# Batch 0 of a fused attention and FFN kernel in another order: x in halves, w_out's quarters right behind w_in's, batch 1 turned in blocks

## The chip, the core and the metric

The kernel runs on one core of a Trainium2 chip. The metric is the device time of one execution in microseconds, the median of the runs; lower is better. A core has five engines with a queue each: TensorE (PE, matrix products, into the PSUM memory of eight banks), VectorE (DVE), ScalarE (ACT), GpSimd (POOL) and SyncE (SP, which issues most of the DMAs here). Each works through its own list in order and waits on semaphores for the others.

## What is computed

```python
# x (8, 8, 512, 64), state (8, 8, 32, 64): batch, head, tokens, width
scores = scale * x @ state^T ; a = softmax(scores)        # rows over 32 states
xread  = a @ state                                        # (8, 8, 512, 64)
scores2 = scale * state @ x^T ; a2 = softmax(scores2)     # rows over 512 tokens
sread  = a2 @ x                                           # (8, 8, 32, 64)
h = concat(xread, sread) as (8 * 544, 512)                # heads side by side
out = elu(h @ w_in) @ w_out        # w_in 512 x 2048, w_out 2048 x 512, float32
```

Each of the 8 batches has 512 token rows and 32 state rows of the FFN's input. All data are float32. In the kernel the raw 64-bit words of the weights are rebuilt into float32 by a few bit operations on ACT and DVE before use.

## The kernel before, in words

**Reassociation.** `a @ state @ w_in` is computed as `a @ (state @ w_in)`: `make_m` (M) makes the small matrix m for a chunk of 512 columns, in two groups `g` of heads, and `ffn1` (F) multiplies it with aT, the turned softmax. So the first FFN product of one of the 16 column blocks `fo` is two matmuls (k = 0, 1) of 128x512, and the second one (`ffn2_row`, O) in batch 0 is four, accumulated over all `fo` in banks 0 to 3. ELU lies between: two ACT steps (`exp_part`, R) and one DVE step (`max_part`, E).

**Batch 0** is written out by hand in `first_batch` as a plan, a string of steps; every engine keeps the order of the plan. The steps that the text names: `x:b.i` turns half i of x of batch b on PE into PSUM (`turn_x`), `xc` copies it out, `sc` makes the scores (`scores`); `mx`, `tr`, `ae`, `tm`, `ps`, `te`, `su`, `pm`, `tt`, `sd` are the two softmaxes, of which `ps` and `pm` are on POOL, `ae` and `te` on ACT, the others on DVE; `tt` makes aT. `sT` and `sTc` turn the other softmax on PE and copy it to aT_s, `sr` is the product a2 @ x (`state_read`), `src` its copy. `w:k.1` and `w:k.2` convert weight tile k, first on ACT, then on DVE. `Z:n` are n products of the identity that nobody reads. `kU` and `kUc` turn and copy the states of the other batches. There are 32 weight tiles of 0.5 MB; `fetch` issues their loads on SP, 7 ahead, and after them x of batch 1 and four DMAs of 1 MB that write the finished w_in to memory (`w_in_mem`), from where later batches read back the part of w_in that is overwritten. Before, the tiles come in the order w_in chunk 0, w_in chunk 1, w_out 0 to 3, w_in chunk 2, and so on. At the end of the plan, batch 1 gets its scores and softmax in the same way as batch 0.

**Batches 1 to 7** run through `batch(b)`: 16 times F and ELU, with make_m for chunks 2 and 3 at `fo` = 5, and then a Strassen scheme (`Strassen`, `Second`) for the second product, whose sums of operands are made on DVE (`whole.sums()`: one written over g_all, then s). Between the Strassen products the hooks run the attention of the next batch: scores (s1), then `move_state`, which turns blocks of 32x32 on DVE into a_blocks and moves them with sixteen DMAs to aT_s, and six products later `state_read`. In these batches x comes in a second form too: `load_blocks` loads 32x32 blocks with sixteen DMAs, and `turn_blocks` turns them on DVE into xT_b. `weight_sum` and `Second.weights` make sums of weights in batch 1; two of the tables lie over the space of w_in's chunks 2 and 3, once these are used and written out.

**Order.** A recording layer, `InOrder`, marks each instruction as kept in program order while its engine's `on` is set; otherwise a scheduler may move it. ACT and POOL are kept for batch 0, SP and PE all the way, DVE (`vector`) up to a line `vector.on = False` in `batch`. x lies in one buffer (`xpool`), so x of a batch can be loaded only after state_read of the one before. Blocks of x, xT of batch 0 and the output tiles share two buffers (`opool`); weight tiles, aT_s, a_blocks, xT_b and the sums share eleven (`work`).

Of the kernel before, what the change touches and what calls it, by code (L numbers as in the profile page):

```python
# [25 lines left out]
def kernel(  # L26
# [103 lines left out]

    x_t, st, m_t = {}, {}, {}

    def load_x(b, engines):
        x_t[b] = xpool.tile([P, R, DM], FP32, name="x_sb")
        x_v = x[b].rearrange("h (p r) d -> p r h d", r=R)
        for r in range(R):
            engines[r % len(engines)].dma_start(
                out=x_t[b][:, r].rearrange("p (h d) -> p h d", d=D), in_=x_v[:, r]
            )

    def load_blocks(b):

# [16 lines left out]
    def turn_blocks(b, m):  # L159

        i, j = divmod(m, 2)
        if j == 0:
            st[b, "xT", i] = work.tile([P, 2, R * P], FP32, tag="w", name="xT_b")
        st[b, m] = st[b, "xT", i][:, j]
        vector.transpose(st[b, m], st[b, "blocks", i][:, j])
# [18 lines left out]
        return raw  # L184

    def turn_states(raw, b0, b1):
        ps = st["k_ps"] = pair(6)[:, :, : (b1 - b0) * 64].rearrange("p t (b q) -> p t b q", q=64)
        for b in range(b1 - b0):
            transpose(ps[:, :, b], raw[:, b].rearrange("p c d -> p (c d)"))

# [14 lines left out]
    def high_words(raw):  # L205
        return raw.bitcast(U32).rearrange("p n (j w) -> p n j w", w=2)[:, :, :, 1]

    def convert_1(dst, raw):

        lo, hi = low_words(raw), high_words(raw)

        scalar.activation(
            out=lo.bitcast(FP32), in_=lo, func=AF.Copy, scale=2.0**-29, bias=2.0**23
        )
        scalar.activation(out=lo, in_=lo.bitcast(FP32), func=AF.Copy, bias=-(2.0**23))


        scalar.activation(out=dst, in_=hi.bitcast(FP32), func=AF.Abs)  # L220

    def convert_2(dst, raw):
        lo, hi = low_words(raw), high_words(raw)
        vector.tensor_scalar(
            out=dst, in0=dst, scalar1=as_float(896 << 20),
            scalar2=as_float((1151 << 20) - 1), op0=ALU.max, op1=ALU.min,
        )

        bits = dst.bitcast(U32)
        vector.tensor_scalar(  # L230
            out=bits, in0=bits, scalar1=3, scalar2=0x3FFFFFF8,
            op0=ALU.logical_shift_left, op1=ALU.bitwise_and,
        )
        vector.scalar_tensor_tensor(
            out=bits, in0=hi, scalar=0xC0000000, in1=bits,
            op0=ALU.bitwise_and, op1=ALU.bitwise_or,
        )
        vector.tensor_tensor(out=bits, in0=bits, in1=lo, op=ALU.add)
# [18 lines left out]
                transpose(ps[:, :, j, r], x_t[b][:, r, m * P : (m + 1) * P])  # L257
        st[b, "xT", i] = ps

    def copy_x(b, i):  # L260
        xT = opool.tile([P, 2, R * P], FP32, tag="o", name="xT")
        for j in range(2):
            st[b, 2 * i + j] = xT[:, j]
            scalar.copy(
                out=xT[:, j].rearrange("p (r t q) -> p t r q", t=2, q=64),
                in_=st[b, "xT", i][:, :, j],
            )

    def by_state(b, rhs, first=6):

# [147 lines left out]
    def make_m(b, c, h=None, first=6):  # L418

        c_in = c if b < 2 else c % 2  # L420
        halves = slice(2 * c_in, 2 * c_in + 2) if h is None else slice(2 * c_in + h, 2 * c_in + h + 1)
        assert h is None or b == 0
        st[b, "m", c] = by_state(b, [w_in[:, halves, m] for m in range(NP)], first)

    def copy_m(b, c, g, copy):
        if g == 0:
            m_t[b, c] = mpool.tile([P, G, 512], FP32, name="m_sb")
        copy(out=m_t[b, c][:, g], in_=st[b, "m", c][:, g])

    def copy_half(b, c, h):  # L430
        if h == 0:
            m_t[b, c] = mpool.tile([P, G, 512], FP32, name="m_sb")
        scalar.copy(
            out=m_t[b, c][:, :, h * 256 : (h + 1) * 256], in_=st[b, "m", c][:, :, :256]
        )

    def exp_part(ps):
# [301 lines left out]
    def first_batch():  # L739
# [4 lines left out]

        plan = """
            kT kTc x:0.0 xc:0.0 x:0.1 w:0.1 xc:0.1 w:0.2 w:1.1 sc:0 Z:14 tr:0.0 tr:0.1 w:2.1 tm:0.0
            tm:0.1 ps:0.0 w:3.1 mx:0.1 mx:0.0 ps:0.1 w:1.2 ae:0.0 te:0.1 ae:0.1 sd:0.0 su:0.1 w:5.1
            M:0.0.0 sd:0.1 pm:0.1 w:3.2 Mc:0.0.0 te:0.0 sT:0 w:4.1 tt:0.1 su:0.0 sTc:0 w:5.2 pm:0.0  # L750
            w:8.1 Z:8 sr:0 tt:0.0 src:0 w:2.2 Z:14 F:0 w:6.1 F:1 w:8.2 R:0 M:0.0.1 R:1 E:0 Mc:0.0.1
            E:1 O:0 w:9.1 w:4.2 w:10.1 w:9.2 F:2 w:7.1 w:6.2 M:0.1.0 F:3 R:2 w:7.2 Mc:0.1.0 O:1
            w:11.1 E:2 R:3 w:10.2 M:0.1.1 w:12.1 F:4 w:11.2 Mc:0.1.1 O:2 R:4 E:3 w:14.1 w:12.2 F:5
            w:13.1 E:4 w:14.2 O:3 R:5 w:16.1 E:5 w:13.2 F:6 w:17.1 w:16.2 M:0.2.0 R:6 F:7 w:18.1
            w:17.2 O:4 Mc:0.2.0 w:18.2 w:20.1 kU w:15.1 E:6 O:5 w:20.2 w:21.1 w:15.2 w:19.1 F:8 kUc
            O:6 R:8 w:21.2 R:7 w:22.1 E:7 M:0.2.1 E:8 F:9 w:19.2 Mc:0.2.1 w:23.1 M:0.3.0 F:10 w:22.2
            w:24.1 O:7 w:23.2 R:9 Mc:0.3.0 E:9 w:25.1 w:24.2 M:0.3.1 F:11 Mc:0.3.1 R:10 w:25.2 O:8
            R:11 E:10 w:26.1 E:11 F:12 w:29.1 w:26.2 O:9 w:30.1 w:29.2 w:27.1 F:13 w:30.2 w:28.1
            O:10 w:27.2 R:13 R:12 w:28.2 x:1.0 w:31.1 O:11 E:12 E:13 xc:1.0 w:31.2 x:1.1 O:12 xc:1.1
            sc:1 O:13 mx:1.1 mx:1.0 ae:1.1 tr:1.0 ae:1.0 tr:1.1 sd:1.0 sT:1 tm:1.0 tm:1.1 ps:1.0  # L760
            F:14 sTc:1 sd:1.1 ps:1.1 te:1.0 sr:1 R:14 su:1.0 F:15 te:1.1 pm:1.0 E:14 src:1 su:1.1
            O:14 R:15 tt:1.0 pm:1.1 E:15 tt:1.1 M:1.0 O:15 Mc:1.0
        """.split()
        make_identity(nc, ident)
        o_ps = [bank(c) for c in range(R)]
        order = [lambda k=k: load_w_in(0, k) for k in range(4)]
        for c in range(1, FC + 1):
            if c < FC:
                order += [lambda c=c, k=k: load_w_in(c, k) for k in range(4)]
            order += [lambda fo=fo: load_w_out(fo) for fo in range(4 * c - 4, 4 * c)]  # L770
        w, h, e = [], {}, {}

        def fetch():
            if len(w) == 12 and len(raw_states) == 1:
                raw_states.append(load_states(1, B))
            if len(w) < len(order):
                w.append(order[len(w)]())
            elif 1 not in x_t:
                load_x(1, [sync])
                for c in range(FC):  # L780
                    k = slice(2 * c, 2 * c + 2)
                    sync.dma_start(out=w_in_mem[:, k], in_=w_in[:, k])

        raw_states = [load_states(0, 1, [sync, scalar])]
        load_x(0, [sync, scalar])
        for k in range(NRAW):
            fetch()
        groups = {
# [8 lines left out]
        for step in plan:  # L797
# [5 lines left out]
                copy_states(*((0, 1) if name == "kTc" else (1, B)))  # L803
            elif name == "Z":
                for i in range(num[0]):
                    matmul(bank(3)[:, :P], ident, ident, start=True, stop=True)
            elif name in groups:
                groups[name](*num)
            elif name in whole:
                whole[name](*num)  # L810
            elif name == "w":
                (convert_1, convert_2)[num[1] - 1](*w[num[0]])
                if num[1] == 2:
                    fetch()
            elif name == "F":
                h[num[0]] = ffn1(0, num[0])
            elif name == "R":
                e[num[0]] = exp_part(h[num[0]])
            elif name == "E":
                max_part(num[0], e[num[0]], h[num[0]])  # L820
            elif name == "O":
                ffn2_row(o_ps, num[0])
            elif name == "x":
                turn_x(*num)
            elif name == "M":
                make_m(*num)
                if len(num) == 2:
                    make_m(1, 1, first=4)
            elif name == "xc":
                copy_x(*num)  # L830
            else:
                assert name == "Mc", step
                if len(num) == 3:
                    copy_half(*num)
                else:
                    for g in range(G):
                        copy_m(*num, g, scalar.copy)
        for g in range(G):
            copy_m(1, 1, g, scalar.copy)

# [6 lines left out]
    def batch(b):  # L847
        if b + 1 < B:
            load_blocks(b + 1)
        for fo in range(FO):  # L850
            elu(ffn1(b, fo), fo)
            if fo > 11 and b + 1 < B:
                turn_blocks(b + 1, fo - 12)
            if fo == FO // 4 + 1:
                for c in (2, 3):
                    make_m(b, c, first=6 if c == 2 else 0)
            if FO // 4 + 1 <= fo < FO // 4 + 5:
                c, g = divmod(fo - FO // 4 - 1, G)
                copy_m(b, 2 + c, g, vector.tensor_copy)
# [1 line left out]
                weight_sum((1, 2, 4, 3)[fo // 4], fo % 4 // 2)  # L861
            if b > 1 and fo == FO // 4 + 2:
                fetch_w_in(0, 0)
        vector.on = False
        nxt = b + 1 < B
        hooks = attention(b + 1) if nxt else [turn_read]
        if nxt and b > 0:
# [9 lines left out]
            used = second  # L877
        whole = Strassen(2, used)
        whole.sums()
        for f in whole.steps():  # L880
            f()
            if hooks:
                hooks.pop(0)()
# [26 lines left out]
                )  # L910

    first_batch()
    load_x(2, [sync])
    for e in (scalar, gpsimd):
        e.on = False
    for b in range(1, B):
# [32 lines left out]
```

## Time and profile before

| | us |
|---|---|
| median of 3 runs | 748.26 (746.68 to 748.34) |
| profiled execution, its own time | 746.17 |
| its span | 744.4 |
| batch 0's scores start on PE | 13.72 |
| first F of batch 0 | 31.96 |
| first F of batch 1 | 128.72 |
| state_read of batch 2 | 189.84 |
| PE, DVE, ACT busy | 723.7, 486.0, 293.3 |
| DMA moved | 76.25 MB |

In the profile all instructions carry line 100, the one in the recording layer's wrapper, so a group is told by its tiles: `ps<-aT,m_sb` is F, `ps<-w_out,g_all` 128x512 is O, `ps<-w_in,kT` is M, `ps<-xT,kT` or `ps<-xT_b,kT` the scores, `ps<-x_sb,aT_s` state_read. A float32 product shows as two records, unless it is a transposition. The records overlap, so durations of one step on PE are best read from start to start: eight records of O take 3.44 from start to start where F follows. Times are in microseconds from the start of the span.

### The profile page before, as it was taken

The numbers are of one execution on the slowest core, as the hardware profiler recorded it, in microseconds if no ns is written. First come the engines' busy times: TensorE is split into PE (matmuls) and PEld (weight loads), VectorE is DVE, ScalarE is ACT, GpSimd is POOL, SyncE is SP. The second block draws the span as 40 slices with busy tenths as digits, with TensorE's granted clock in tenths as the row PEclk, the third lists the DMA queues.
The fourth block names the chain that finished last, engine by engine and source line by source line (L and its number), as shares of the span: only waits on it lengthen the run. The fifth ranks groups of instructions, "written<-read, shape, count | busy, mean of one in ns | idle before, by whom it ended". The sixth has DMA issues, their size and how long they took to land.

```text
span 744.4 us, 11377 instructions
## 1 busy us (share of the span) xinstructions
PE 723.7 (97%) x4472; PEld 502.5 (68%) x4472; DVE 486.0 (65%) x892; ACT 293.3 (39%) x539; POOL 34.4 (5%) x38
## 2 busy tenths in 40 slices
PE   4899999989999999999999999999999999999998
PEld 2544444348874798469944896479746894699886
DVE  2999975799437883677556864787367845556231
ACT  5899955542126311651055203621264106400420
POOL 0100002002000200010000200020002000000000
PEclk9999999999999999999999999999999999999999
DMA  9667900801634063503461164307340403003000
GB/s 282 225 201 239 326 0 1 167 4 22 177 94 133 5 179 84 160 1 106 122 153 46 26 173 110 116 13 187 83 144 1 143 33 137 1 1 142 29 4 25
DMA packets 126366, 76.25 MB, mean 102 GB/s; under 512 B 113768, under 2 KB 114280, under 8 KB 122472
## 3 DMA queue, kind: packets, MB, share of 16 engines
q1 hardware_dynamic: 124004, 74.90, 34.8%
q10 hardware_dynamic: 2308, 0.62, 0.4%
q8 instruction: 35, 0.57, 0.3%
q14 instruction: 19, 0.16, 0.1%
HBM read 59.24 MB, written 13.11 MB: 97 GB/s over the span
## 4 chain that ended last, share of the span: by engine, by line
PE 89%; DVE 6%; SPq 1%; DMA 1%; ACT 1%; issue 1%; POOL 0%; ACTq 0%; DVEq 0%; POOLq 0%
PE ps L100 89%; DVE w_in L100 2%; SPq L100 1%; DMA x_sb<-in_x_dram 1%; DVE g_all L100 1%; DVE total_t L100 0%; DVE s L100 0%; DVE top L100 0%; DVE w_out L100 0%; ACT e_sb L100 0%; POOL t_sb L100 0%; ACT xT L100 0%; DVE xT_b L100 0%; DVE aT L100 0%; DVE t_sb L100 0%
## 5 line engine op out<-in xcount | busy, mean ns | idle before, releaser
L100 PE MATMUL ps<-w_out,g_all 128*128 128x256 f32 (+2 forms) x1088 | 232.5, 366 | 1.1 <-DVE g_all L100 0.8
L100 PE MATMUL ps<-aT,m_sb 128*128 128x512 f32 x512 | 226.3, 595 | 1.1 <-DVE m_sb L100 0.8
L100 PEld LDWEIGHTS ps<-w_out,g_all 128*128 128x128 f32 x1088 | 176.6, 191 | 53.5 <-issue 37.1
L100 PEld LDWEIGHTS ps<-aT,m_sb 128*128 128x128 f32 x512 | 95.4, 190 | 122.0 <-issue 109.1
L100 ACT ACTIVATE e_sb<-ps 128x512 f32<-128x512 f32 (+1 forms) x144 | 82.5, 573 | 220.4 <-PE ps L100 205.1
L100 DVE SCALAR_TENSOR_TENSOR g_all<-e_sb,ps 128x512 f32<-128x512 f32 (+1 forms) x144 | 94.2, 656 | 101.0 <-ACT e_sb L100 100.4
L100 DVE TENSOR_TENSOR o_sb<-o_sb,ps 128x128 f32<-128x128 f32 (+2 forms) x170 | 52.6, 310 | 75.2 <-PE ps L100 73.5
L100 ACT ACTIVATE e_sb<-e_sb 128x512 f32<-128x512 f32 (+1 forms) x144 | 87.3, 606 | 4.6
L100 PE MATMUL ps<-t_w,s 128*128 128x256 f32 (+1 forms) x480 | 88.8, 339 | 0.0
L100 PEld LDWEIGHTS ps<-t_w,s 128*128 128x128 f32 x480 | 77.6, 191 | 8.1 <-DVE o_sb L100 0.2
L100 ACT COPY o_sb<-ps 128x512 f32<-128x512 f32 (+2 forms) x52 | 20.6, 424 | 151.7 <-PE ps L100 144.6
L100 ACT ACTIVATE raw<-raw 128x512 f32<-128x512 uint32 x64 | 43.7, 683 | 1.0
L100 DVE TENSOR_TENSOR s<-s,g_all 128x512 f32<-128x512 f32 (+1 forms) x36 | 32.2, 897 | 15.9 <-PE ps L100 15.5
L100 POOL TENSOR_TENSOR t_sb<-t_sb,top_t 128x512 f32<-128x512 f32 x16 | 16.7, 1047 | 517.0 <-DVE top_t L100 517.0
L100 DVE TENSOR_TENSOR g_all<-g_all,s 128x512 f32<-128x512 f32 (+1 forms) x36 | 32.1, 891 | 9.6 <-PE ps L100 9.6
L100 PE MATMUL ps<-w_in,kT 64*32 64x512 f32 (+1 forms) x576 | 34.0, 547 | 0.9 <-ACT a_s L100 0.9
L100 DVE TENSOR_TENSOR g_all<-g_all 128x512 f32<-128x512 f32 (+1 forms) x36 | 32.2, 894 | 0.5
L100 DVE TENSOR_TENSOR s<-g_all 128x512 f32<-128x512 f32 (+1 forms) x36 | 31.6, 883 | 0.8 <-DMA aT_s<-a_blocks 0.4
L100 PE MATMUL ps<-t_w,g_all 128*128 128x128 f32 (+1 forms) x240 | 32.1, 282 | 0.0
L100 PE MATMUL ps<-w_in,s 128*128 128x128 f32 x240 | 31.2, 277 | 0.0
L100 PEld LDWEIGHTS ps<-t_w,g_all 128*128 128x128 f32 x240 | 29.8, 192 | 0.5
L100 PEld LDWEIGHTS ps<-w_in,s 128*128 128x128 f32 x240 | 28.7, 192 | 0.6 <-DVE o_sb L100 0.5
(86 smaller groups left out, 557.1 us busy)
## 6 DMA issues: line engine op xcount, KB each, us to landing
w_in<-w_in_mem SPq DMA_DIRECT2D x26, 1024.0 KB, 5.9
raw<-in_moe_w_in_dram SPq DMA_DIRECT2D x16, 512.0 KB, 4.6
raw<-in_moe_w_out_dram SPq DMA_DIRECT2D x16, 512.0 KB, 4.5
out_dram<-o_sb SPq DMA_DIRECT2D x16, 512.0 KB, 2.8
x_sb<-in_x_dram SPq DMA_DIRECT2D x30, 256.0 KB, 4.9
x_blocks<-in_x_dram SPq DMA_DIRECT2D x96, 64.0 KB, 2.4
w_in_mem<-w_in SPq DMA_DIRECT2D x4, 1024.0 KB, 8.3
aT_s<-a_blocks SPq DMA_DIRECT2D x96, 32.0 KB, 1.9
```

What stands on the lines that cost most here:

```text
L100: ins = getattr(self.engine, name)(*args, **kw)
```

## The change

The diff reorders batch 0 and what belongs to it:

- x of batch 0 is loaded in two halves by head (`parts=2`), all eight DMAs on SP and ACT, four each, ahead of the weights. Half 0 is turned into banks 4 and 5, half 1 into banks 0 and 1; of each half, one part is copied by ACT (`xc`) and the other by DVE (`xd`).
- The plan is a new one. The weight tiles come as w_in chunk c, then w_out 4c to 4c+3. make_m for chunks 2 and 3 is one step each and no longer two halves.
- Batch 1 in the plan is no longer turned on PE: x comes as blocks (`load_blocks`, `bt`), and its state softmax goes through `move_state` (`ab`). Its state_read moves into `batch(1)` at `fo` = 5, ahead of make_m for chunks 2 and 3; x of batch 2 is loaded behind it.
- The four writes of w_in_mem move from `fetch` to the end of the plan, which on SP is behind the sixteen DMAs of batch 1's aT_s.
- `vector.on = False` moves down, behind `whole.sums()`, so that the first sums of batch 1's Strassen scheme stay behind the last `turn_blocks` on DVE.
- The conversion is split into named functions with the same instructions.

```diff
-    def load_x(b, engines):
+    def load_x(b, engines, parts=1):
...
+        n = H // parts
+        for i in range(parts):
+            for r in range(R):
+                engines[r % len(engines)].dma_start(
+                    out=x_t[b][:, r, i * n * D : (i + 1) * n * D].rearrange(
+                        "p (h d) -> p h d", d=D
+                    ),
+                    in_=x_v[:, r, i * n : (i + 1) * n],
+                )
...
-        ps = st["k_ps"] = pair(6)[:, :, : (b1 - b0) * 64]...
+        ps = st["k_ps"] = pair(2 if b0 else 6)[:, :, : (b1 - b0) * 64]...
...
-    def copy_x(b, i):
...
+    def copy_x(b, i, j, copy):
+        if (b, "xT_sb", i) not in st:
+            st[b, "xT_sb", i] = opool.tile([P, 2, R * P], FP32, tag="o", name="xT")
+        st[b, 2 * i + j] = xT = st[b, "xT_sb", i][:, j]
+        copy(
+            out=xT.rearrange("p (r t q) -> p t r q", t=2, q=64), in_=st[b, "xT", i][:, :, j]
+        )
...
         plan = """
-            kT kTc x:0.0 xc:0.0 x:0.1 w:0.1 xc:0.1 w:0.2 w:1.1 sc:0 Z:14 tr:0.0 tr:0.1 w:2.1 tm:0.0
-            tm:0.1 ps:0.0 w:3.1 mx:0.1 mx:0.0 ps:0.1 w:1.2 ae:0.0 te:0.1 ae:0.1 sd:0.0 su:0.1 w:5.1
-            M:0.0.0 sd:0.1 pm:0.1 w:3.2 Mc:0.0.0 te:0.0 sT:0 w:4.1 tt:0.1 su:0.0 sTc:0 w:5.2 pm:0.0
-            w:8.1 Z:8 sr:0 tt:0.0 src:0 w:2.2 Z:14 F:0 w:6.1 F:1 w:8.2 R:0 M:0.0.1 R:1 E:0 Mc:0.0.1
-            E:1 O:0 w:9.1 w:4.2 w:10.1 w:9.2 F:2 w:7.1 w:6.2 M:0.1.0 F:3 R:2 w:7.2 Mc:0.1.0 O:1
...
+            kT kTc x:0.0 xd:0.0 xc:0.0 x:0.1 xd:0.1 xc:0.1 sc:0 w:0.1 mx:0.0 tr:0.0 ae:0.0 tr:0.1
+            w:1.1 tm:0.0 sd:0.0 ps:0.0 tm:0.1 w:0.2 ps:0.1 te:0.0 w:2.1 su:0.0 te:0.1 mx:0.1 pm:0.0
+            w:3.1 su:0.1 tt:0.0 pm:0.1 ae:0.1 w:1.2 w:4.1 Z:16 sT:0 sd:0.1 M:0.0.0 sTc:0 tt:0.1
+            w:4.2 Mc:0.0.0 sr:0 w:7.1 Z:8 F:0 w:2.2 w:8.1 F:1 w:3.2 R:0 R:1 E:0 M:0.0.1 w:9.1 E:1
+            w:8.2 Mc:0.0.1 src:0 F:2 w:9.2 w:6.1 F:3 w:7.2 R:2 kU R:3 M:0.1.0 kUc w:5.1 E:3 O:0 E:2
+            Mc:0.1.0 w:5.2 w:11.1 F:4 w:6.2 w:10.1 O:1 w:12.1 w:11.2 R:4 w:12.2 F:5 w:13.1 E:4 O:2
+            w:10.2 w:14.1 R:5 w:13.2 M:0.1.1 w:16.1 O:3 E:5 w:14.2 Mc:0.1.1 w:17.1 F:6 w:16.2 w:18.1
+            O:4 w:17.2 R:6 w:19.1 E:6 F:7 w:18.2 w:15.1 O:5 w:19.2 R:7 w:21.1 w:15.2 M:0.2 O:6
...
+            w:25.2 O:10 R:11 w:28.2 w:30.1 M:0.3 E:11 w:31.1 w:30.2 O:11 Mc:0.3 w:31.2 w:29.1 F:12
+            bt:1.1 bt:1.2 R:12 F:13 bt:1.3 bt:1.0 E:12 sc:1 R:13 w:29.2 O:12 mx:1.1 E:13 ae:1.1
+            tr:1.0 F:14 sd:1.1 tm:1.0 tr:1.1 ps:1.0 O:13 R:14 mx:1.0 te:1.0 E:14 ae:1.0 su:1.0
+            tm:1.1 pm:1.0 F:15 ab:1 ps:1.1 O:14 R:15 tt:1.0 sd:1.0 te:1.1 E:15 su:1.1 pm:1.1 M:1.0
+            tt:1.1 O:15 Mc:1.0
         """.split()
...
-        order = [lambda k=k: load_w_in(0, k) for k in range(4)]
-        for c in range(1, FC + 1):
-            if c < FC:
-                order += [lambda c=c, k=k: load_w_in(c, k) for k in range(4)]
-            order += [lambda fo=fo: load_w_out(fo) for fo in range(4 * c - 4, 4 * c)]
+        order = []
+        for c in range(FC):
+            order += [lambda c=c, k=k: load_w_in(c, k) for k in range(4)]
+            order += [lambda fo=fo: load_w_out(fo) for fo in range(4 * c, 4 * c + 4)]
...
             elif 1 not in x_t:
+                load_blocks(1)
                 load_x(1, [sync])
-                for c in range(FC):
-                    k = slice(2 * c, 2 * c + 2)
-                    sync.dma_start(out=w_in_mem[:, k], in_=w_in[:, k])
 
         raw_states = [load_states(0, 1, [sync, scalar])]
-        load_x(0, [sync, scalar])
+        load_x(0, [sync, scalar], 2)
...
             elif name == "x":
-                turn_x(*num)
+                turn_x(*num, first=4 - 4 * num[1])
+            elif name == "bt":
+                turn_blocks(*num)
+            elif name == "ab":
+                move_state(*num)
             elif name == "M":
-                make_m(*num)
-                if len(num) == 2:
+                make_m(*num, first=0 if num[:2] == [0, 0] else 6)
+                if num[0] == 1:
                     make_m(1, 1, first=4)
...
+        for c in range(FC):
+            k = slice(2 * c, 2 * c + 2)
+            sync.dma_start(out=w_in_mem[:, k], in_=w_in[:, k])
         for g in range(G):
             copy_m(1, 1, g, scalar.copy)
...
             if fo == FO // 4 + 1:
+                if b == 1:
+                    state_read(1)
+                    keep_read(1)
+                    load_x(2, [sync])
                 for c in (2, 3):
-                    make_m(b, c, first=6 if c == 2 else 0)
+                    make_m(b, c, first=0 if (c == 2) == (b == 1) else 6)
...
-        vector.on = False
         nxt = b + 1 < B
...
         whole.sums()
+        vector.on = False
...
     first_batch()
-    load_x(2, [sync])
```

## The prediction

> **What bounds the kernel now.** The page first: TensorE (PE) is busy 97% of the span, so an edit counts only where it shortens PE's list or fills one of its gaps.
>
> ```profile
> PE 723.7 (97%) x4472; PEld 502.5 (68%) x4472; DVE 486.0 (65%) x892; ACT 293.3 (39%) x539; POOL 34.4 (5%) x38
> PE   4899999989999999999999999999999999999998
> DVE  2999975799437883677556864787367845556231
> ```
>
> The slices show two more things: PE is open only at the start, and VectorE (DVE) is full in slices 2 to 5, batch 0. The table of busy time by stretch confirms that for 40 to 50 us, where PE is full too:
>
> ```profile
> 40.00:50.00 10.00, 10.00 (x53) 3.91 (x52) 9.55 (x19) 9.84 (x17) 0.00 (x0) 1.00 0.65 211
> ```
>
> Then the timeline of PE, for the gaps (start, length, what, count; the bracket is the idle time before):
>
> ```profile
> 13.72 1.96 PE L100 MATMUL ps<-xT,kT 64*32 64x512 f32 x16 [1.67 <-ACT xT L100]
> 31.96 3.70 PE L100 MATMUL ps<-aT,m_sb 128*128 128x512 f32 x8 [0.34 <-DVE aT L100]
> 37.05 3.70 PE L100 MATMUL ps<-w_out,g_all 128*128 128x512 f32 x8 [0.79 <-DVE g_all L100]
> 128.72 10.46 PE L100 MATMUL ps<-aT,m_sb 128*128 128x512 f32 x24
> 166.23 0.62 PE L100 MATMUL ps<-xT_b,kT 64*32 64x512 f32 x2 [2.32 <-DVE xT_b L100]
> 189.84 1.10 PE L100 MATMUL ps<-x_sb,aT_s 128*32 128x64 f32 x64
> ```
>
> Scores of batch 0 start at 13.72, the first FFN product (F:0) at 31.96, batch 1 at 128.72; the gaps after F:0 are 0.79, 0.76 (at 146.31) and 2.32. The last line is state_read of batch 2. The chain of waits holds PE without a break from 166.23 for 400 us, but two timelines show how little spare that last line had:
>
> ```profile
> 165.47 0.70 DVE L100 STREAM_TRANSPOSE xT_b<-x_blocks 128x512 f32<-128x512 f32 x1
> 167.31 0.69 DVE L100 TENSOR_REDUCE top<-ps 128x1 f32<-128x512 f32 x1
> 176.40 0.65 DVE L100 STREAM_TRANSPOSE a_blocks<-a_s 128x512 f32<-128x512 f32 x1
> ```
>
> ```profile
> 80.21 4.21 SPq L100 DMA_DIRECT2D w_in_mem<-w_in  x4
> 177.12 10.43 SPq L100 DMA_DIRECT2D aT_s<-a_blocks  x16
> ```
>
> Batch 2's softmax starts at 167.31, its sixteen DMAs end about 1.9 us after 186.9, at 188.85: 1.0 us before PE reads them.
>
> **What the Trainium skill says.** *TensorE: Matmul & The Clock Gate*, part 1 (the HAM clock gate): an idle window of about 3.4 us puts PE at half clock. The trace agrees in kind: the first scores take 1.96 us, the same work at 109.68 takes 1.09. *SBUF — State Buffer*, "Who interferes with whom": a 2-port DVE operation and a GpSimd one exclude each other. The trace agrees: the first two conversion steps take 0.88 us, but 1.59 at 23.62, beside a GpSimd subtraction or scaling. *DMA: Bandwidth & Descriptors*, "Issuing engines are not separate DMA queues": all transfers share 16 engines, so x ahead of the weights gets the rate that both have now.
>
> **The change, part by part.** Durations: the DVE half of a weight (w.2) 2.25 us, the ACT half (w.1) 1.86, F 1.71 to 1.73, O 3.44, max part (E) 0.60, exp part 1.15.
>
> 1. *Start.* x goes as halves, all eight issues ahead of the weights (two more on SP and two on ACT, about 0.6 us each). 1.1 MB at the rates of the view of DMA queues over the first 60 us (slices of 1.5 us: 195, 257, 222 GB/s from 3 us on) has landed, an estimate, at about 8.2 instead of 8.98. The turned halves go to different banks, so the second no longer waits for the first's copy, and the copies run on DVE and ACT together, with w:0.1 behind them: transposes to 8.95, copies to 9.6, scores to 11.0 instead of 15.68. Gain 4.7 (3 to 5).
>
> 2. *Softmax to the last aT.* Before, 15.84 to 31.91 = 16.1 us of DVE, three weights within. After: maxima 2 x 0.75, transposes 2 x 0.63, row maxima 2 x 0.60, totals 0.63, sums 2 x 1.1, aT 2 x 0.61, two weights 4.5, about 1.5 for GpSimd's lock: 14.0, ending at 25.0. F:0 is not at 25.0: PE does make_m (24.9), state_read 1.1 and eight warm-up products of 0.24 (28 records in 3.39 us at 28.23, two records each): 27.9, against 31.96. PE is empty from the sixteen warm-ups' end (about 16.2) to the second exponential (20.5): if that halves its clock, F:0 is at 29.5.
>
> 3. *F:0 to M:0.2.* M:0.0.1 waits for weight 3 (25.05 + 3 x 2.25 = 31.8), and its copy sits on ACT behind R:1 and w:9.1: F:2 at 35.0, a new PE gap of 2.5. From there DVE sets the pace, with full covers on ACT: M:0.2 needs weight 19, so 17 weights x 2.25, 7 E x 0.60, kUc 1.0 and 0.25 of waiting for R:1 = 43.7; 25.05 + 43.7 = 68.7. PE, rolled forward beside it, is done with O:5 at 68.3.
>
> 4. *M:0.2 to batch 1.* PE alone: 10 O 34.4, 8 F 13.7, two whole M 2.1, scores 1.1, M:1.0 1.95, changes of shape about 0.7: 54.0, ending at 122.6 against 128.72. Gone from PE here: turn_x of batch 1 (2 x 0.73) and turn_state (1.0); state_read (1.1) moves on. The four block transposes (2.5) and a_blocks (1.25) are new on DVE, where over 3 us are free then; 32 more DMA issues on SP lie in time in which it only waited. Gain 6.1.
>
> 5. *Batch 1 to state_read of batch 2*, in us after batch 1's first product. Before: 61.1. After: six F 10.4, state_read of batch 1 1.1, first M 1.0 = 12.5; then DVE's list to the fourth xT_b: four m_sb copies 2.4, ten E 6.0, four transposes 2.5, five 1024-wide sums 5.6, nine 512-wide ones 6.1, together 22.6, and 1.0 of waits for exponentials: 36.1 (scores hoped for it at 34.5). The DVE stays in program order one step longer, so the sums now stand between that transpose and batch 2's maximum: 1.13 + 2.26 + 2.26 = 5.65, where before one piece of 1.1 stood. Maximum at 41.75, landing 21.5 later as before (167.31 to 188.85): 63.3. PE would be there at 60.8. So the 2.32 stall is not removed; 1.6 of it stays at the scores and about 2.5 comes back at state_read. Loss 2.2 (0.5 to 3.5).
>
> 6. *Costed at nothing.* The writes of w_in_mem, moved from 80 us to behind batch 1's aT_s: a_blocks ends 9.3 us before batch 1 by DVE's list, sixteen issues of 0.655 follow, so SP reaches the writes 1.2 us into batch 1; three of four MB have landed by 11 (12.5 us for all four before, with other traffic), and DVE overwrites w_in first at 12.5. load_x of batch 2 and stores: some 5 us to spare. Batches 2 to 7 are the same lists.
>
> Sum against the profiled execution (746.17, span 744.4): 6.1 - 2.2 = 3.9, less 0.4 (1.5 us of half clock at about 3 in 10): 3.5. The median shown is 748.26, 2.1 above that execution; I take the same difference from it: 744.8.
>
> **Rivals.** (a) *Chain of batch 2 in time*: if DVE has the sums done while PE is still in its first products, only state_read's 1.1 is paid: gain 5 to 6, 742.5. For it: DVE had idle pieces of 1.0 between E's before 141. Against: none from 141 to 167. (b) *The start gives little*: half clock, x or the first weight landing 1 us late, a few GpSimd locks: F:0 at 30.5, and since DVE waits for R:1 all its weights move too; gain 0 to 1.5, 747.3. (c) *Slower*: w_in_mem. The DVE overwrite of w_in waits for the third MB, and the m_sb copies of batch 1 stand behind it; each us past 12.5 delays batch 2's softmax by one. It decides from a landing at about 16, and passes 0.3% slower at 18.7 and more: 751. For it: SP issues in order behind sixteen aT_s. Against: a_blocks would have to come 8 us later than I find. (d) *Not what it says*: the halves might land no sooner than whole rows; that is case (b).
>
> **How the numbers follow.** Forecast 0.42, (a) 0.15, (b) 0.27, (c) 0.16. 0.3%, 2.2 us, is about what a measurement of this kernel tells from no change. Faster by more: most of the forecast's case and (a), 0.52; within: the forecast's upper end and most of (b), 0.29; slower 0.19. Range 741.2 to 749.4: (a)'s better end to the start of (c).
>
> **What would show it.** Scores of batch 0 ending near 11, F:0 near 28, F:2 near 35 behind an ACT copy, batch 1 at 123, a stall of 1 to 2 us at batch 2's scores, and one before its state_read with a DMA as releaser. Wrong if F:0 is later than 30.5, if PE has gaps between 40 and 120, or if DVE is seen waiting for w_in_mem.

## The result, and the profile after

The changed kernel takes 748.84 us, the median of 4 runs (748.41 to 750.2), beside 748.3 for the kernel before: ratio 1.0016, 95% interval 1.0 to 1.0033. No difference beyond what can be measured, where a gain of 3.5 us was forecast. The profiled execution took 748.82, its span 747.0: 2.6 more than the span before. It is the likeliest number that failed; what came is near rival (b), with one cost that no rival had. Three runs of the experiments (one of e1, two of e4) took 1527 to 2350 us, and no ratio below counts them.

The page of after: one line of busy time, the slices of PE and DVE.

```profile
PE 723.2 (97%) x4376; PEld 500.9 (67%) x4376; DVE 490.4 (66%) x900; ACT 289.7 (39%) x531; POOL 34.3 (5%) x38
PE   6699999999899999999999999999999999999998
DVE  3899995799337783677556863787377845556230
```

PE has 96 records fewer, as the change says, and yet is busy only 0.5 us less, since part of its list runs at half speed. And the 8 that was in the ninth slice before, the stall at batch 2's scores, now stands in the eleventh, at batch 2's state_read. The timeline of PE (start, length, what, count, idle time before and its releaser):

```profile
9.94 3.41 PE L100 MATMUL ps<-xT,kT 64*32 64x512 f32 x16
23.07 1.12 PE L100 MATMUL ps<-ident,a_s 128*128 128x128 f32 x4 [5.32 <-ACT a_s L100]
31.92 3.60 PE L100 MATMUL ps<-aT,m_sb 128*128 128x512 f32 x8
39.15 3.70 PE L100 MATMUL ps<-aT,m_sb 128*128 128x512 f32 x8 [3.04 <-ACT m_sb L100]
126.82 10.46 PE L100 MATMUL ps<-aT,m_sb 128*128 128x512 f32 x24
161.31 2.51 PE L100 MATMUL ps<-xT_b,kT 64*32 64x512 f32 x14
165.89 10.63 PE L100 MATMUL ps<-w_out,g_all 128*128 128x256 f32 x48
187.73 0.27 PE L100 MATMUL ps<-x_sb,aT_s 128*32 128x64 f32 x2 [0.61 <-DMA aT_s<-a_blocks]
190.34 1.12 PE L100 MATMUL ps<-x_sb,aT_s 128*32 128x64 f32 x58 [2.35 <-DMA aT_s<-a_blocks]
191.40 5.29 PE L100 MATMUL ps<-w_out,g_all 128*128 128x256 f32 x16
```

The first scores start at 9.94 instead of 13.72, but F:0 at 31.92, as before (31.96). Batch 1 starts at 126.82, 1.9 earlier; I call that time T0. The 2.32 of idle time in batch 2's scores (166.23 before) no longer shows, but the scores and the two M behind them still take 4.58 from start to start (161.31 to 165.89). Where they wait for nothing, in e5 below, they take 2.73, so some 1.9 are lost there, hidden in overlapping records. Inside state_read(2) PE is idle for 2.96 (0.61 and 2.35), with the DMAs as releaser. The last line is a new cost: these sixteen records take 5.12 from start to start, the same work before 3.55 (190.88 to 194.43). The table by stretch of after, with PE's granted clock as the third column from the end, says why:

```profile
26.00:28.00 2.00, 1.49 (x28) 0.68 (x32) 1.93 (x6) 0.34 (x1) 0.00 (x0) 0.50 0.22 36
192.00:194.00 2.00, 2.00 (x6) 1.65 (x5) 0.35 (x1) 0.00 (x0) 0.00 (x0) 0.50 1.00 397
```

Half clock, both at the start and behind the new wait. DVE's timeline shows what the late F:0 costs, two waits for its exponentials (R:0 and R:1):

```profile
35.13 0.69 DVE L100 SCALAR_TENSOR_TENSOR g_all<-e_sb,ps 128x512 f32<-128x512 f32 x1 [1.08 <-ACT e_sb L100]
36.84 0.69 DVE L100 SCALAR_TENSOR_TENSOR g_all<-e_sb,ps 128x512 f32<-128x512 f32 x1 [1.03 <-ACT e_sb L100]
```

F:0 of batch 2 comes at 215.93, that is T0+89.1, where before it was T0+85.1 (213.84). Sum: -1.9 at T0, +2.4 to the end of the wait, +1.6 of half clock behind it, +0.5 in the rest: +2.6.

### The profile page after: what moved, and what is told of

It is laid out like the page before. It is cut to its first block, busy times and chain, and to the rows that moved or that the text cites. A ratio compares the mean times of both kernels' runs of the same rounds, so it can differ in the third digit from the quotient of the medians.

```text
span 747.0 us, 11237 instructions
## 1 busy us (share of the span) xinstructions
PE 723.2 (97%) x4376; PEld 500.9 (67%) x4376; DVE 490.4 (66%) x900; ACT 289.7 (39%) x531; POOL 34.3 (5%) x38
## 4 chain that ended last, share of the span: by engine, by line
PE 85%; DVE 8%; SPq 2%; DMA 2%; ACT 1%; issue 1%; POOL 0%; DVEq 0%; POOLq 0%
PE ps L100 85%; SPq L100 2%; DVE w_in L100 1%; DVE w_out L100 1%; DVE g_all L100 1%; DMA x_sb<-in_x_dram 1%; DVE total_t L100 1%; DMA aT_s<-a_blocks 1%; DVE top L100 1%; DVE s L100 1%; ACT e_sb L100 0%; DVE t_sb L100 0%; DVE top_t L100 0%; DMA raw<-in_moe_w_out_dram 0%; DMA s_first<-in_state_dram 0%
```

## The experiments

Runs of one kernel spread over 2 us and more, so the verdicts rest on places in the traces, counted from T0 where the start plays no part. The "kernel before" in each ratio ran on the same chip; its medians were 747.96 to 748.33. A ratio is worked out from the whole sets of runs and is not the quotient of the two medians.

### Batch 2's late softmax: e1, e9, e5, e10

**e1: the place of the sums.** The prediction held that the Strassen sums, now kept behind the last xT_b, make batch 2's maximum late.

```diff
+        vector.on = False
         nxt = b + 1 < B
...
         whole.sums()
-        vector.on = False
```

> The changed kernel (profile: batch 1 starts at 126.8, batch 2's maximum 41.9 us later, its aT_s lands 63.5 us later, end 747.0) with one part undone: vector.on = False stands ahead of whole.sums() again. Theory 1 (DVE's whole list up to batch 2's maximum is too long, because four weight sums are scheduled ahead of it, 2.6 us; where the operand sums stand among them makes no difference): batch 2's maximum stays at 41.5 to 42.5 us after batch 1's start, PE waits at the scores (up to 6 us) and no longer at state_read; time 748 to 749.5, no gain. Theory 2, the one in the prediction (the sums ahead of the maximum are the cause): maximum at 38 to 39.5, state_read in time, 745.5 to 746.5.

Measured: 750.2, ratio 1.0047 (1.003 to 1.0064). F of batch 2 at T0+89.5: no gain. The timelines of DVE and PE of e1:

```profile
159.89 0.68 DVE L100 TENSOR_TENSOR t_w<-t_w 128x512 f32<-128x512 f32 x1
...
161.09 0.68 DVE L100 TENSOR_TENSOR w_in<-w_out 128x512 f32<-128x512 f32 x1
...
167.86 0.69 DVE L100 TENSOR_REDUCE top<-ps 128x1 f32<-128x512 f32 x1 [0.90 <-PE ps L100]
```

```profile
165.91 1.06 PE L100 MATMUL ps<-xT_b,kT 64*32 64x512 f32 x2 [2.41 <-DVE xT_b L100]
```

The stall only goes back to the scores (1.29 and this 2.41), and state_read(2) starts at 191.10, T0+65.5, without a wait. Either way the maximum is at T0+42: the scheduler, left free, also puts the sums ahead of it, and DVE is busy for 35.5 us from T0 to the maximum in both kernels. So the moved line is not what makes it late. Among that work are pieces of 0.6 us like the first two lines, which belong to the second level's weights, written for much later in the program. Nine of them, 5.4 us in all, stand ahead of the maximum in the changed kernel and in e1, five in the kernel before, whose maximum was at T0+38.6. Why it is four more is not shown; what they cost is e5's question.

**e9: what state_read(2) waits for.** Half of its sixteen DMAs go to another issuer.

```diff
-                sync.dma_start(
+                (scalar if b == 2 and q % 2 else sync).dma_start(
                     out=st[b, "aT_s"][q * 32 : ...
```

> The changed kernel with one edit: of the sixteen DMAs of aT_s for batch 2, every second one is issued by ACT instead of SP (each takes its issuer about 0.65 us, sixteen in a row 10.4). Nothing is left out. Theory 1 (state_read(2) waits only for the last of these issues, and the half clock behind it comes only from that wait): with T0 the start of batch 1, they have landed by about T0+58.3 instead of T0+63.5, PE comes at T0+60.0 and does not wait, the clock stays at 1.0, F(2,0) at T0+84.5 instead of T0+89.1, total about 4.5 less, 744.3. Rival (another queue's issues or ACT's copies behind them, or the transfers' bandwidth, decide): state_read(2) still stalls by over 1 us or o_sb copies on ACT come late and stall a product by over 1; F(2,0) at T0+87 or later.

Measured: 744.24, ratio 0.9959 (0.9947 to 0.9972); F of batch 2 at 210.43, T0+84.0. The timelines of SP, ACT and PE of e9:

```profile
178.13 5.21 SPq L100 DMA_DIRECT2D aT_s<-a_blocks  x8
```

```profile
178.09 5.58 ACTq L100 DMA_DIRECT2D aT_s<-a_blocks  x8
```

```profile
186.43 1.10 PE L100 MATMUL ps<-x_sb,aT_s 128*32 128x64 f32 x64
187.46 3.72 PE L100 MATMUL ps<-w_out,g_all 128*128 128x256 f32 x16
```

No wait, and no half clock behind it: the sixteen records that took 5.12 take 3.56 (the next start is at 191.02). Nothing else was touched, and 5.1 us of T0+89.1 are gone, 4.6 in the medians. They are 3.6 within state_read (4.59 from start to start, now 1.03) and 1.6 behind it. This is the main finding: the stall and the cold clock, and so the loss in batch 2, hung on 10.4 us of issuing in one queue. The Trainium skill, *DMA: Bandwidth & Descriptors*, "Issuing engines are not separate DMA queues", says that issuing from several engines saves only the time that it takes to initiate a DMA, "usually small relative to the DMA itself". The first half agrees; the second doesn't here: 0.65 us of issuing for each 32 KB transfer, which lands 1.9 us after its issue, so sixteen in a row are nearly all issuing.

**e5 and e10: the weights behind the softmax.** e5 keeps DVE in program order through all of batch 1, with a_blocks ahead of aT:

```diff
         whole.sums()
-        vector.on = False
         for f in whole.steps():
...
+        vector.on = False
         for i in (1, 0):
             store(b, i, whole.o_sb[i])
```

> Batch 1's DVE work stays in program order up to its stores (the switch to free order moves behind all of its Strassen steps), and batch 2's a_blocks are turned ahead of its aT. So the 0.6 us pieces of the second level's weights (w_in<-t_w, t<-t_w, w_in<-w_out and the like, nine of them, 5.4 us, found ahead of batch 2's maximum in the changed kernel's timeline) go behind it. Nothing is left out. Theory 1 (that hoisted work, not the place of the sums, makes batch 2's softmax late): with T0 the start of batch 1, the maximum at T0+36.5 to 37 instead of T0+41.9, the aT_s landing by about T0+61, no stall before state_read(2) (2.96 before), no half clock behind it (1.6 before); F(2,0) at T0+84.5 instead of T0+89.1, total 4 to 4.6 less, about 744.3. Rival (the DMAs of aT_s or the softmax's own order decide): the maximum earlier but state_read(2) still stalled by 2 or more, F(2,0) at T0+87 or later, total within 1.5 of the changed kernel.

Measured: 754.61, ratio 1.0095 (1.0069 to 1.012): worse. PE and DVE of e5:

```profile
187.77 1.89 PE L100 MATMUL ps<-x_sb,aT_s 128*32 128x64 f32 x58 [2.34 <-DMA aT_s<-a_blocks]
...
206.52 2.08 PE L100 MATMUL ps<-t,s 128*128 128x128 f32 x8 [3.78 <-DVE o_sb L100]
```

```profile
194.70 0.69 DVE L100 TENSOR_TENSOR o_sb<-o_sb,ps 128x512 f32<-128x512 f32 x1 [12.24 <-ACT o_sb L100]
```

The maximum came 2.5 earlier (165.82, T0+39.4), not the 5 that I expected: up to it DVE is busy 5.4 us less (30.1 for 35.5), but idle 2.9 more, so the rest of the moved pieces had filled pauses. But PE's scores no longer waited either, so PE was at state_read(2) at T0+58.1, and the DMAs, landed at T0+61.3, stalled it still. And what stands in order behind an addition that needs PE's product waits with it: DVE is idle for 12.24, and PE then pays 3.78 and, further on, 1.45. Both theories fall in part; the order is right up to the softmax and wrong behind it.

So e10 keeps order up to the end of the softmax, a_blocks ahead of aT as in e5, lets the weights follow in order, frees the rest, and splits the DMAs as e9:

```diff
+            def late(i, b):
+                vector.on = True
+                second[i].weights(b)
+                vector.on = False
...
         whole.sums()
-        vector.on = False
         for f in whole.steps():
             f()
             if hooks:
                 hooks.pop(0)()
+                vector.on = False
```

> As the run before, and on DVE the order is kept through batch 2's softmax, a_blocks ahead of aT, with the second level's weights kept in order behind it (free order for the rest), so that PE's scores of batch 2 no longer wait for late xT_b either. Theory 1: scores of batch 2 without a stall as in the run with batch 1 wholly in order (PE at state_read(2) at T0+58.1), aT_s landed by T0+56.5, F(2,0) at T0+82.7, total about 742.4. Rival (the weights, now late, hold the second-level products, as in that run's stalls of 3.78 and 1.45): stalls of 1 us or more at products 128x128, F(2,0) at T0+84.5 or later, no better than the split alone.

Measured: 743.63, ratio 0.994 (0.9923 to 0.9957). F of batch 2 at 209.81, T0+83.0, state_read(2) at T0+58.1 without a wait, and one stall of 0.60 behind it: 6.1 us less than the changed kernel from T0, where 6.4 were expected. Against e9 that is 1.0 less from T0. The median gains only 0.6 on e9: T0 is 0.4 later in this profile, in which PE fell to half clock at F:2 (F:2 and F:3 took 5.33 from start to start, not 3.63), which belongs to the start.

### The half clock behind the wait: e4

Fourteen products that nobody reads, ahead of state_read(2), keep PE at work through the first of the wait.

```diff
+        if b == 1:
+            read_2 = hooks[6]
+            hooks[6] = lambda: (
+                [matmul(bank(3)[:, :P], ident, ident, start=True, stop=True) for i in range(14)], read_2()
+            )
```

> The changed kernel with fourteen unread products of the identity (3.4 us) on PE ahead of batch 2's state_read, in the place where it waits 3 us for aT_s. Theory 1 (after that wait PE runs at half clock for about 3.4 us, which costs 1.6 more): state_read ends at 191.4 as before, the following 128x256 products take 3.5 instead of 5.1 us, time 747.2. Rival (the clock record only reflects the idle time, and costs nothing): 748.8 or a little more.

Measured: 749.01, ratio 1.0016 (1.0006 to 1.0026). PE of e4:

```profile
191.51 1.05 PE L100 MATMUL ps<-x_sb,aT_s 128*32 128x64 f32 x58 [1.03 <-DMA aT_s<-a_blocks]
192.50 3.72 PE L100 MATMUL ps<-w_out,g_all 128*128 128x256 f32 x16
```

The clock stays at 1.0 and the sixteen records take 3.56 (the next start at 196.06), so with PE kept at work the half clock does not come. The mean clock of the runs agrees: 0.992 or 0.993 in thirteen of e4's, where three of the changed kernel's four have 0.991. F of batch 2 is at T0+88.4, 0.7 of the 1.6 won: in this execution the DMAs landed 0.9 later, for a reason that the trace doesn't show, and with stalls of 1.01 and 0.85 in later batches, where the changed kernel has one of 0.44, the total shows nothing.

### The start: e3, e2, e7, e6, e11

**e3: copies by bank.** `copy_x` splits a half of x between ACT and DVE by the PSUM bank (t) instead of by j, which lies in both banks.

```diff
-            out=xT.rearrange("p (r t q) -> p t r q", t=2, q=64), in_=st[b, "xT", i][:, :, j]
+            out=st[b, "xT_sb", i].rearrange("p j (r t q) -> p t j r q", t=2, q=64)[:, t],
+            in_=st[b, "xT", i][:, t],
```

> The changed kernel with the two copies of a turned half of x split by PSUM bank and no longer by half of each bank, so that ACT reads one bank and DVE the other. Theory 1 (ACT's copy waits for DVE's because both read the same banks): the copies run side by side, ACT's start 0.7 us earlier, batch 0's scores end at 12.6 instead of 13.3, DVE's chain and batch 1 start 0.6 earlier (126.2), time 748.2. Rival (the copies wait for each other because of the tile that they write): no change, scores at 13.3, 748.8.

Measured: 752.11, ratio 1.0045 (1.0022 to 1.0068). ACT's copy for the first half, in the changed kernel and then in e3:

```profile
8.50 0.58 ACT L100 COPY xT<-ps 128x512 f32<-128x512 f32 x1 [3.18 <-DVE xT L100]
```

```profile
7.67 0.59 ACT L100 COPY xT<-ps 128x512 f32<-128x512 f32 x1 [2.35 <-PE ps L100]
```

In the changed kernel ACT waits for DVE's copy of the same banks, although both only read. The Trainium skill has this: *PSUM — Partial Sum Buffer*, "PSUM bank collisions raise a hardware error", wants two engines on one bank ordered, two readers included. By bank they run side by side, though they still write one tile, and the first maximum is at 12.85 instead of 13.43. So the copies cost 0.6. In the profiled execution the total is worse for another reason, PE of e3:

```profile
38.98 6.52 PE L100 MATMUL ps<-aT,m_sb 128*128 128x512 f32 x8 [3.04 <-ACT m_sb L100]
```

F:2 and F:3 at half speed, 6.45 from start to start instead of 3.63, behind the same gap of 3.04 that left the clock alone in the changed kernel's profile. Eight of the traces have this gap, of 3.04 or 3.05: it left the clock alone in six (the changed kernel, e1, e2, e4, e5, e9) and halved it in two (e3, e10). e9's runs show what may be the two cases in numbers: twelve of 743.78 to 744.92, mean clock 0.991 to 0.993, and six of 746.73 to 747.93, at 0.988 or 0.989. The Trainium skill, *TensorE: Matmul & The Clock Gate*, part 1, says that the window of some 3.4 us is free-running, and that the number of slow products at a kernel's start so differs from run to run. A gap that sometimes cools PE fits that in kind, though it is shorter than the idle window that the page names, and e2's below is shorter still. Of these eighteen only one of the twelve was traced, with F:2 at full speed; that the six are the other case is an inference.

**e2: more products of the identity ahead of sT** (`Z:38` for `Z:16` in the plan).

> The changed kernel with Z:16 made Z:38, so that PE is not empty from 17.7 to 23.1 us. Theory 1 (PE falls to half clock in that gap, and state_read and the eight warm-up products then run at half speed): granted clock 1.0 from 20 to 32 us instead of 0.5, F:0 at 30.1 instead of 31.9, DVE waits 2 us less for the exponentials, batch 1 at 124.8 instead of 126.8, time 746.8. Rival (DVE sets the start, PE's clock hides behind it): clock 1.0 but batch 1 within 0.5 of 126.8, time 748.8.

Measured: 749.2, ratio 1.0019 (1.0007 to 1.0031). F:0 at 31.33. The table by stretch of e2:

```profile
24.00:26.00 2.00, 0.10 (x4) 0.00 (x0) 1.90 (x4) 1.63 (x4) 0.01 (x1) 1.00 0.00 0
26.00:28.00 2.00, 1.74 (x64) 1.33 (x68) 1.90 (x7) 1.04 (x2) 0.00 (x0) 0.79 0.34 70
28.00:30.00 2.00, 2.00 (x27) 1.83 (x20) 1.93 (x4) 1.94 (x4) 0.00 (x0) 0.50 0.66 222
```

The clock is full until the next pause, of 2.15, in which M:0.0.0 waits for DVE, and falls then to 0.50. The warm-up of eight products ahead of F:0 still ran at half speed at first. One gap filled was not enough; it says nothing yet on what a warm start is worth.

**e7: one step of the plan moved,** `Mc:0.0.1` ahead of `w:9.1`.

> Only one step of the plan moves: the copy Mc:0.0.1 ahead of w:9.1 on ACT. Theory 1 (from F:0 on DVE's list sets the pace, PE's gap before F:2 costs nothing as long as the clock holds): F:2 at about 37.4 instead of 39.15, the gap about 1.3 instead of 3.04, but batch 1 within 0.5 of 126.8 and the total unchanged, 748.8. Rival (that gap is lost time, as the prediction's step 3 counts F:2): batch 1 1.5 or more earlier, total about 747.2.

Measured: 749.06, ratio 1.0016 (1.0007 to 1.0024). F:2 at 36.59 (39.15), the gap ahead of it 1.23, T0 126.08; F:0 was 0.75 earlier in this execution, most of it from an earlier x (the first maximum came 0.45 earlier), and T0 is 0.74 earlier. So 1.8 us less of gap are worth nothing: from F:0 on DVE's list decides, as step 3 has it.

**e6 and e11: the pauses filled.** Z:38 ahead of sT, ten products between the halves of M:0.0.0, none ahead of F:0, eight behind F:1, five behind M:0.0.1. In e6 they land in bank 5, where F:1's values lie, so that the ones behind F:1 replace them ahead of R:1 (that group of columns is lost); in e11 in bank 3.

```diff
-            ... w:4.1 Z:16 sT:0 ... w:7.1 Z:8 F:0 w:2.2 w:8.1 F:1 w:3.2 ... M:0.0.1 w:9.1
+            ... w:4.1 Z:38 sT:0 ... w:7.1 F:0 w:2.2 w:8.1 F:1 Z:8 w:3.2 ... M:0.0.1 Z:5 w:9.1
...
+            if m == 1:
+                for i in range(fill):
+                    matmul(bank(3)[:, :P], ident, ident, start=True, stop=True)
```

> PE is kept at work through the start with products of the identity that nothing reads: 38 instead of 16 ahead of sT, 10 between the two halves of M:0.0.0, none ahead of F:0 (8 before), 8 behind F:1, 5 behind M:0.0.1. Theory 1 (half clock costs the start its gain): granted clock 1.0 from 17 to 40, state_read about 1.1 (1.93 before), F:0 at 28 to 28.5 instead of 31.92, DVE no longer waits for R:0 and R:1 (2.1 us before), so batch 1 starts about 2 us earlier, at 124.6 to 125.2, and the total falls by about 2, to 746.8. Rival (the start is set by DVE and ACT lists, so PE's clock matters little): F:0 earlier, but batch 1 within 0.7 of 126.8 and the total unchanged.

> The filled start once more, with all unread products in PSUM bank 3 instead of 5. In the run in bank 5 the eight behind F:1 overwrote F:1's values and held R:1 back, and DVE waited 1.51 for it. Theory 1: with R:1 free, that wait goes too, F:0 at about 28 and batch 1 at 124.6 to 125.2 where the changed kernel has 126.8; total 746.8. Rival (DVE's list from 28 us on sets batch 1 whatever F:0 does): batch 1 within 0.7 of 125.6 to 126.8, total 747.5 or more.

Measured: e6 747.14, ratio 0.9995 (0.9986 to 1.0005), T0 125.58; e11 745.75, ratio 0.9966 (0.9958 to 0.9974), T0 124.22, x landing within 0.3 of the changed kernel's. The table and PE of e11:

```profile
20.00:40.00 20.00, 19.57 (x195) 13.36 (x195) 19.14 (x40) 17.77 (x34) 2.10 (x2) 1.00 0.62 194
```

```profile
28.08 3.70 PE L100 MATMUL ps<-aT,m_sb 128*128 128x512 f32 x8
```

The mean clock from 20 to 40 is 1.0 (0.74 in the changed kernel), state_read takes 1.03 from start to start (27.05 to 28.08) instead of 1.87, and F:0 comes at 28.08. With it DVE's waits for R:0 and R:1 go (1.08 and 1.03; in e6 one of 1.51 stayed, for the R:1 that was held back), and T0 falls by 2.6, 3.1 in the medians.

Not all of this is the clock, for the edit also takes away the eight products ahead of F:0. In the changed kernel they took 2.53 from start to start, up to F:0 at 31.92:

```profile
29.39 2.69 PE L100 MATMUL ps<-ident 128*128 128x128 f32 x16
```

At full clock, in the kernel before, they took 1.93 (25.22 to 27.15). So of the 3.8 by which F:0 is earlier, about 1.9 are the products left out, 0.3 an earlier x, and 1.6 the clock. That 28.08 is near the prediction's 27.9, which has the eight products in it, is luck. With them at full clock F:0 would come at about 30.0 and DVE would still wait some 0.6 for R:1, an estimate from the distance of F:0 to these waits in the changed kernel; some 1.5 of the 2.1 are then the clock's. No run fills the pauses and keeps the eight products.

### All together: e8 and e12

e8 joins the edits of e5, e6, e7 and e3; e12 those of e10, e11, e7 and e3; both go without the five products behind M:0.0.1.

> The three edits above together (DVE's order through batch 1, the filled start, Mc:0.0.1 first) and the xT copies of DVE and ACT split by PSUM bank instead of by half. Theory 1: the gains add, since they lie in different stages: 2 to 2.7 at the start, 4 to 4.6 from batch 1 to batch 2; batch 1 starts at about 124.3, F(2,0) at about 208.8, total about 742, below both kernels. Rival (what is gained at the start is given back as a wait later, for weights or for the second batch's chain): total above 744.5, with a stall of 1 us or more between F:0 and batch 2's first product that neither single edit shows.

> All together: the filled start in bank 3, xT copies by bank, Mc:0.0.1 first, batch 2's softmax kept in order with the weights behind it, its aT_s DMAs on two queues. Theory 1: the gains add: batch 1 at about 124.5, F(2,0) at about 207.3 (changed kernel 215.9), total 740 to 741, about 1% below both kernels. Rival (the gain of one stage is given back as a wait in a later one): total above 743.5, with stalls of 1 us or more between batches 2 and 7 that the changed kernel doesn't have.

Measured: e8 (F:1's group lost, as in e6) 750.51, ratio 1.0044 (1.0027 to 1.0061): T0 fell to 124.74, and e5's stalls of 3.78 and 1.45 took it back. e12: 739.11 (738.98 to 739.18, 4 runs), ratio 0.988 (0.9864 to 0.9896). PE of e12:

```profile
123.58 10.46 PE L100 MATMUL ps<-aT,m_sb 128*128 128x512 f32 x24
...
181.71 1.10 PE L100 MATMUL ps<-x_sb,aT_s 128*32 128x64 f32 x64
...
206.57 10.46 PE L100 MATMUL ps<-aT,m_sb 128*128 128x512 f32 x24
```

T0 is 3.2 earlier than in the changed kernel, F of batch 2 9.4 (T0+83.0 as in e10), the span 9.6, with clock 1.0 throughout. The gains add, for each lies in a stage of its own: 2.6 at the start (e11) and 6.1 from batch 1 to 2 (e10); the 0.6 that is left, e12's T0 against e11's, goes to the copies by bank and Mc together. It is 1.2% below the kernel before and 1.3% below the changed one.

## Why the prediction was wrong, point by point

What failed is the price of half clock, and the size of step 1. The sum held 0.4 for half clock, 1.5 at 3 in 10, and only ahead of F:0; it cost about 1.5 there and 1.6 more behind state_read(2), where no term stood for it. Step 1 gained 2.4 instead of 4.7.

**Step 1, the start: wrong in size.** "The copies run on DVE and ACT together": they ran one after the other, for they read the same bank (e3: 0.6). The last part of x reached PE at 9.11, 0.9 later than the 8.2 of the estimate and no sooner than the whole rows before (8.98), which is rival (d); in the experiments it was there between 8.29 and 9.30. "Scores to 11.0": they ended at 13.3. The 0.8 that x and the copies leave open fit the scores themselves, whose records took 1.06 each, against 0.60 for the same work at 109.68 before; that this is half clock is not shown, since the clock column reads 1.00 from 10 to 14. The gain was 2.4 instead of 4.7.

**Step 2, softmax to the last aT: right in DVE's part, wrong in PE's.** DVE took 13.8 from the maximum to the last aT (13.43 to 27.25), 14.0 predicted. "F:0 at 27.9": 31.92, later even than the branch "if that halves its clock, 29.5". The branch was named and given 3 in 10; it was the case, because PE stood still for 5.32. Its price, 1.6, was about right: F:0 came 4.7 behind the last aT, where the prediction had 2.9 without half clock, and e11 leaves 1.6 for the clock. Its chance was too low, and with it that of what rival (b) says of it, that DVE then waits for R:1. Of the 4.2 that T0 missed, 2.2 stand already at the last aT, 27.25 for 25.05, from step 1; 1.9 are those waits, 2.1 for 0.25.

**Step 3: its mechanism right.** F:2 came behind ACT's copy, after a gap of 3.04 (2.5 predicted), and DVE's list set the pace from there; the wait for R:0 and R:1 was 2.1 and not 0.25, as F:0 was late. M:0.2 at 72.92, 68.7 predicted: all of that difference came from steps 1 and 2 and this wait.

**Step 4: right.** M:0.2 to batch 1 took 53.9, 54.0 predicted; no gaps of PE there.

**Step 5: right number and path, wrong cause.** 63.5 from T0 to the end of the wait, 63.3 predicted; 1.9 lost at the scores, 1.6 predicted; and the stall at state_read came, with DMAs as releaser. DVE's list was right too, the nine 512-wide pieces (6.1 in it) included: maximum at T0+41.9, 41.75 predicted. But the place of `whole.sums()`, on which the loss was put, is not what makes it late: e1 frees them again and gains nothing. Four more pieces of the second level's weights than before stand ahead of the maximum, and moved behind it, all nine give back 2.5 (e5). That a wait can be taken away at its last link, the sixteen issues, was not seen.

**Not in the prediction at all:** the half clock behind that wait, 1.6 us (gone in e4 and e9), the largest part of what was missed from T0 on; 0.2 are the wait itself, and 0.5 lie behind batch 2's first F and were not followed up.

**Step 6: right.** w_in_mem was issued at 128.30 and no DVE instruction waited for it; rival (c) did not happen. Rival (b) did, with F:0 still later than it said. In its own terms the sum was 6.1 - 2.2 - 0.4; measured, 1.9 - 2.4 - 1.6 - 0.5.

**Against the medians.** I carried the profiled execution's distance to the median, 2.1, over to the new kernel. It was 0.0 there, and the median of before also holds runs with a lower mean clock (in the experiments' runs of it 0.995 to 0.998 where they take about 748, 1.0 where they take about 746, as in its profile); the medians differ by 0.5 and the spans by 2.6. Such a distance is no constant of a kernel.

## What to carry to other kernels

Price a pause of PE twice: once as waiting, and once as the half clock of what follows, which may be more (at F:2 the pause was worth nothing in e7, and half clock behind it 2.8 in e3); and where a plan leaves pauses of 2 to 5 us, fill all of them with unread products or shorten them, for a single filled one gave no gain here (e2). When an engine's list shrinks, look for the last link of the wait that remains: here it was neither a product nor a sum but one queue's issuing of many small DMAs, which a second queue halves. Where a scheduler orders instructions, read what stands ahead of the critical one in the trace, and hold the rest behind it only up to the point where it is done.

## What the runs showed of the hardware that I had not expected

- The same gap of 3.04 us ahead of F:2 halved PE's clock in two traces and not in six, and the same wait of 2.61 in state_read(2) (0.27 and 2.34) halved it in e5 and not in e8. Filling the pauses at the start (e11) raised the mean clock but did not end the spread, 3.5 us in twenty runs; e12, without the wait at state_read(2) too, shows 0.2 in four.
- In the changed kernel the half clock behind the wait at state_read(2) began 0.9 us after PE had work again and lasted 3.4: the granted clock is 0.98 at 191.0 to 191.2, 0.50 from 191.2 to 194.6, and 0.99 at 194.6 to 194.8.
- Short products with pauses did not warm PE up: sT, M:0.0.0 and state_read, busy 5 of the 6.3 us from 23.07 to 29.39, all ran at 0.50 in the changed kernel.
- Sixteen DMAs of 32 KB took SP 10.4 us to issue, and eight on each of two queues 5.2 and 5.6, while the time to land stayed at 1.9 us.
